# Batch 1's head pairs 2 and 3 transposed by DMA instead of TensorE, with the schedule around them moved

## The chip, the cores and the metric

The kernel runs on one core of one Trainium2 chip. The metric is the device time of one execution in microseconds (us), the median of several runs. The kernel before takes 240.53 us (three runs, 240.4 to 240.64). The profile that is read below is of one execution with a span of 239.1 us.

Engines have these names in the profile: PE is TensorE's matmul, PEld its weight load, DVE is VectorE, ACT is ScalarE, POOL is GpSimd and SP is SyncE. POOL and SP also issue DMA transfers, and each of those queues is worked through in order.

## The reference

An attention with a local window and eight global keys, and behind it a gated feed-forward block over all 3072 tokens.

```python
def _attn_ref(q, k, v, n_global, n_local):
    B, H, S, D = q.shape                      # 4, 8, 768, 64
    scores = np.matmul(q, k.transpose(0, 1, 3, 2)) / np.sqrt(D)
    pos = np.arange(S)
    rel = pos[:, None] - pos[None, :]
    is_global = pos[None, :] < n_global       # the first 8 keys
    is_local = (rel >= 0) & (rel < n_local)   # the last 96 keys up to the query
    keep = is_global | is_local
    dist = np.where(is_global & ~is_local, n_local, np.abs(rel))
    slopes = 2.0 ** (-8.0 * (np.arange(H) + 1) / H)
    scores = scores - slopes[:, None, None] * dist
    scores = np.where(keep, scores, -1e9)
    a = softmax(scores)                       # max, exp, sum written out in the reference
    return np.matmul(a, v)

def _moe_ref(x, w_gate, w_val, w_out):        # x: 3072 x 512, the heads side by side
    g = x @ w_gate                            # 512 x 1536
    return (g / (1 + np.exp(-g)) * (x @ w_val)) @ w_out
```

The inputs and the output are float32; the kernel computes in float16 with float32 sums.

## The kernel before

The feed-forward block is the bulk of the work. It is cut into 8 tiles of 384 tokens, two tiles per batch. A tile has 12 steps f = 0 to 11; each step computes a gate product (`gps`, 4 matmuls) and a value product (`vps`, 4 matmuls), and tanh, two multiplies and a store into `hT` follow on ACT and DVE. The product with `w_out` is cut into "output pieces" of 3 matmuls (`ops`): four pieces make one block of 128 tokens, and the last of the four is followed by ACT's copy and SP's store.

The attention of the next batch is computed between the steps of the current tiles. A head pair needs its queries and keys with the head dimension on the partitions (`qT`, `kT`), so both are transposed. For batch 1 TensorE does that: batches 2 and 3 have it done by DMA.

```python
# the staging of q and k: two layouts, "tokens (p j)" for TensorE, rows for the DMA transpose
    def stage(b):
        qst[b] = sb2.tile([128, H, J * D], FP16, name="qst", tag="qst")
        kst[b] = sb2.tile([128, H, J * D], FP16, name="kst", tag="kst")

    def load_qk(b, h0, h1):
        for st, src in ((kst[b], k), (qst[b], q)):
            nc.gpsimd.dma_start(
                out=st[:, h0:h1, :],
                in_=src[b, h0:h1].rearrange("h (p j) d -> p h (j d)", p=128))

    def stage_rows(b):
        qst[b] = sb2.tile([128, NP, J, 2, D], FP16, name="qst", tag="qst")
        kst[b] = sb2.tile([128, NP, J, 2, D], FP16, name="kst", tag="kst")
        kend[b] = sb2.tile([128, H, D], FP16, name="kend", tag="kend", bufs=1)
        nc.gpsimd.memset(kend[b], 0.0)
        nc.sync.dma_start(out=kend[b][0:NG], in_=kG[:, b - 1])
        for hp in range(NP):
            pair = kG[:, b - 1, 2 * hp:2 * hp + 2, :].rearrange("p h d -> p (h d)")
            nc.sync.dma_start(
                out=kst[b][0:NG, hp].rearrange("p t e d -> p t (e d)"),
                in_=pair.unsqueeze(1).broadcast_to([NG, J, 2 * D]))

    def load_v_rest(b, c):
        n = min(KC, S - KC * c)
        nc.gpsimd.dma_start(
            out=vSs[b][NG:NG + n, c, :, :],
            in_=v[b, :, KC * c:KC * c + n, :].rearrange("h p d -> p h d"))
# ... cut ...
    def load_rows(b, i, h):
        st, src = ((qst, q), (kst, k))[i]
        p0, n = ((0, 128), (NG, KC))[i]
        nc.gpsimd.dma_start(
            out=st[b][p0:p0 + n, h // 2, :, h % 2, :],
            in_=src[b, h, 0:n * J].rearrange("(t p) d -> p t d", p=n))

    def load_ends(b):
        nc.gpsimd.dma_start(
            out=kend[b][NG:NG + S - KC * J],
            in_=k[b, :, KC * J:S, :].rearrange("h p d -> p h d"))

    def turn_ends(b):
        nc.sync.dma_start_transpose(out=kE, in_=kend[b].rearrange("p h d -> p (h d)"))
```

A pair transposed by TensorE (12 transposes for q and 12 for k; copies to SBUF on ACT and DVE), and one transposed by DMA:

```python
        def transposes(self):
            b, hp = self.b, self.hp
            trq, trk = (t[:, 0:S] for t in banks("trs", FP16))
            for st, tr in ((kst[b], trk), (qst[b], trq)):
                for j in range(J):
                    for hi in range(2):
                        nc.tensor.transpose(
                            tr[64 * hi:64 * hi + 64, 128 * j:128 * j + 128],
                            st[:, 2 * hp + hi, D * j:D * j + D], ident)
            self.qT = sb2.tile([128, S], FP16, name="qT", tag="qT", bufs=NP)
            self.kT = kTs[hp]
            k3 = self.kT.rearrange("r (c m) -> r c m", m=128)
            t3 = trk.rearrange("r (j p) -> r p j", j=J)
            for c0, c1, n in ((0, 6, KC), (6, 7, S - 6 * KC)):
                nc.scalar.copy(
                    out=k3[:, c0:c1, NG:NG + n].rearrange("r c (p j) -> r c p j", j=J),
                    in_=t3[:, 20 * c0:20 * c0 + (c1 - c0) * (n // J), :].rearrange(
                        "r (c p) j -> r c p j", c=c1 - c0))
            nc.vector.tensor_copy(
                out=self.qT.rearrange("r (p j) -> r p j", j=J),
                in_=trq.rearrange("r (j p) -> r p j", j=J))
            nc.vector.tensor_copy(
                out=k3[:, :, 0:NG],
                in_=k3[:, 0, NG:2 * NG].unsqueeze(1).broadcast_to([128, NCH, NG]))
# ... cut ...

        def transposes_dma(self):
            b, hp = self.b, self.hp
            self.qT = sb2.tile([128, S], FP16, name="qT", tag="qT", bufs=NP)
            self.kT = kTs[hp]
            for dst, st in ((self.kT[:, 0:S], kst), (self.qT, qst)):
                nc.sync.dma_start_transpose(
                    out=dst.rearrange("r (t p) -> r t p", t=J),
                    in_=st[b][:, hp].rearrange("p t e d -> p (t e d)"))
```

The scores of a pair and the weighted values of four heads, which are called below `sc` and `va`:

```python
            hp = self.hp
            for c in range(NCH):
                cb, col, q0, n = chunks[c]
                if cb != bk:
                    continue
                for hi in range(2):
                    r = slice(64 * hi, 64 * hi + 64)
                    keys = (kE[r, hp, :] if c == J and self.b > 1
                            else self.kT[r, 128 * c:128 * c + 128])
                    nc.tensor.matmul(
                        sc[hi][:, col:col + n], lhsT=keys,
                        rhs=self.qT[r, q0:q0 + n], start=True, stop=True)
        # ... cut: exps (ACT) and mask (DVE or POOL) ...
# ... cut ...

        def x_out(self, half, side):
            return x_of(2 * self.b + half)[:, 2 * self.g + side, :]

        def values(self, half, bank, mul_eng):
            den = bank("den")
            self.weigh(half, den, None)
            srcs = []
            for side in range(2):
            # ... cut: ns copied out on ACT; invert, spread and two scale steps put off to DVE ...
```

The order of the loads on POOL's queue up to batch 1, and the schedule. `(t, f)` names a step of a tile; what stands at `(t, f)` is emitted after the gate, value and output pieces of that step, and `(t, f, n)` before its output piece n.

```python
    for c in range(3, NCH):
        load_v_rest(0, c)
    load_w(wg, 8)
    load_w(wv, 8)
    load_wo(0)
    load_wo(1)
    load_wo(2)
    stage(1)
    load_qk(1, 0, 4)
    load_globals()
    load_wo(3)
    load_qk(1, 4, 8)
    for c in range(NCH):
        load_v_rest(1, c)
# ... cut ...
    def fetch(b, *hps):
        def step():
            for hp in hps:
                pairs[b, hp].transposes_dma()
            if hps[0] > 0:
                turn_ends(b)
        return step

    def first(t, b):
        return {(t, 2): [tr(b, 0), tr(b, 1)],
                (t, 4): [sc(b, (0, 0), (0, 1), (1, 0))],
                (t, 5): [tr(b, 2), tr(b, 3)],
                (t, 6): [sc(b, (1, 1), (2, 0), (2, 1))],
                (t, 8): [sc(b, (3, 0), (3, 1))],
                (t, 9): [va(b, 0, 0)],
                (t, 10, 1): [va(b, 1, 0), lambda: run_later(len(later))]}

    def both(t, b):

        n = b + 1
        return {(t, 0): [sc(b, (0, 2), (1, 2), (2, 2)), fetch(n, 0, 1)],
                (t, 5): [sc(b, (3, 2), (0, 0, n), (1, 0, n)), fetch(n, 2, 3)],
                (t, 8): [vas(b, 1)],
                (t + 1, 0): [sc(n, (0, 1), (1, 1), (2, 0))],
                (t + 1, 4): [sc(n, (2, 1), (3, 0), (3, 1))],
                (t + 1, 8): [vas(n, 0)]}
# ... cut: n_out is the repeating list of how many output pieces a step has ...
    def ff(t, f0, f1, n_out=(0,)):
        return [(t, f, n_out[(f - f0) % len(n_out)]) for f in range(f0, f1)]

    stretches = [
        (ff(0, 9, 10) + ff(0, 10, 12, (1,)), {}),
        (ff(1, 0, 6, (1, 0, 0, 1, 1, 2)) + ff(1, 6, 10, (1, 1, 1, 0)) + ff(1, 10, 12, (2,)), first(1, 1)),
        (ff(2, 0, 12, (1,)) + ff(3, 0, 12, (1,)), both(2, 1)),
        (ff(4, 0, 12, (1,)) + ff(5, 0, 12, (1,)), both(4, 2)),
        (ff(6, 0, 12, (1,)), second(6, 3)),
        (ff(7, 0, 10, (1,)) + ff(7, 10, 12), {})]
# ... cut ...
    at_step(1, 7, lambda: [copy_globals(b) for b in range(1, B)])
    for b, base, rate, v_at in ((2, 20, 2.0, (31, 32, 33, 34, 35, 36, 37)), (3, 38, 1.4, (56, 57, 58, 59, 60, 61, 62))):
        items = [(base, lambda b=b: stage_rows(b)), (base + 1, lambda b=b: load_ends(b))]
        n = 0
        for hp in range(NP):
            for i in (1, 0):
                for e in range(2):
                    items.append((base + n / rate,
                                  lambda b=b, i=i, h=2 * hp + e: load_rows(b, i, h)))
                    n += 1
        items += [(at, lambda b=b, c=c: load_v_rest(b, c)) for c, at in enumerate(v_at)]
        for when, it in items:
            at_step(int(when) // NFF, int(when) % NFF, it)
```

Of the kernel before, what the change touches and what calls it, by code (L numbers as in the profile page):

```python
# [10 lines left out]
FP16 = mybir.dt.float16  # L11
# [26 lines left out]
def kernel(  # L38
# [14 lines left out]
    B, H, S, D = q.shape  # L53
    NG, NL = int(n_global), int(n_local)
    assert (B, H, S, D) == (4, 8, 768, 64)
    assert (NG, NL) == (8, 96)
    NP = H // 2
# [5 lines left out]
    J = S // 128  # L63
    NCH = 7
# [26 lines left out]
    sb2 = ctx.enter_context(tc.tile_pool(name="sb2", bufs=2))  # L91
# [50 lines left out]
    qst, kst, kend = {}, {}, {}  # L142
    kE = sb.tile([128, NP, 128], FP16, name="kE")
# [9 lines that stand above are left out]
                in_=src[b, h0:h1].rearrange("h (p j) d -> p h (j d)", p=128))  # L153

    def stage_rows(b):
        qst[b] = sb2.tile([128, NP, J, 2, D], FP16, name="qst", tag="qst")
        kst[b] = sb2.tile([128, NP, J, 2, D], FP16, name="kst", tag="kst")
        kend[b] = sb2.tile([128, H, D], FP16, name="kend", tag="kend", bufs=1)
        nc.gpsimd.memset(kend[b], 0.0)
        nc.sync.dma_start(out=kend[b][0:NG], in_=kG[:, b - 1])  # L160
        for hp in range(NP):
            pair = kG[:, b - 1, 2 * hp:2 * hp + 2, :].rearrange("p h d -> p (h d)")
            nc.sync.dma_start(
                out=kst[b][0:NG, hp].rearrange("p t e d -> p t (e d)"),
                in_=pair.unsqueeze(1).broadcast_to([NG, J, 2 * D]))

    def load_v_rest(b, c):
# [4 lines that stand above are left out]
# [11 lines left out]
    def copy_globals(b, c0=0):  # L183
        nc.sync.dma_start(
            out=vSs[b][0:NG, c0:],
            in_=vG[:, b, :, :].unsqueeze(1).broadcast_to([NG, NCH - c0, H, D]))


    def load_rows(b, i, h):
        st, src = ((qst, q), (kst, k))[i]  # L190
        p0, n = ((0, 128), (NG, KC))[i]
        nc.gpsimd.dma_start(  # L192
            out=st[b][p0:p0 + n, h // 2, :, h % 2, :],
            in_=src[b, h, 0:n * J].rearrange("(t p) d -> p t d", p=n))

    def load_ends(b):
# [3 lines that stand above are left out]
# [15 lines left out]
    def load_wo(g):  # L215
        nc.gpsimd.dma_start(
            out=wo[:, 3 * g:3 * g + 3, :],
            in_=moe_w_out[384 * g:384 * g + 384].rearrange("(f p) d -> p f d", p=128))
# [18 lines left out]
    def banks(name, dt=FP32):  # L237
        return [bank(name, dt) for _ in range(2)]

    def spare(name, dt=FP32):  # L240
        tag = state["x"][gv.get("n", 0) % len(state["x"])]
        gv["n"] = gv.get("n", 0) + 1
        return single(name, tag, dt)
# [9 lines left out]
    later = []  # L253

    def run_later(n):
        for _ in range(n):
            if later:
                later.pop(0)()

    class Pair:  # L260
# [114 lines left out]
        def scores(self, bk, mul_eng, sc):  # L375
# [4 lines that stand above are left out]
                    continue  # L380
                for hi in range(2):
                    r = slice(64 * hi, 64 * hi + 64)
                    keys = (kE[r, hp, :] if c == J and self.b > 1
                            else self.kT[r, 128 * c:128 * c + 128])
                    nc.tensor.matmul(  # L385
                        sc[hi][:, col:col + n], lhsT=keys,
                        rhs=self.qT[r, q0:q0 + n], start=True, stop=True)
            at = sb2.tile([128, 2, BANK], FP16, name="at", tag=f"at{bk}", bufs=NP)
            self.at[bk] = at

            def exps():
                for hi in range(2):
                    nc.scalar.activation(out=at[:, hi, :], in_=sc[hi][:, 0:BANK],  # L393
                                         func=AF.Exp, scale=scale)

            def mask():
                m = masks[:, 2 * hp:2 * hp + 2, :]
                if bk == 1:
                    for i in range(2):
                        a2 = at[:, :, WIN * i:WIN * i + WIN]  # L400
                        mul_eng.tensor_mul(a2, a2, m[:, :, WIN:2 * WIN])  # L401
                else:
                    o = WIN // 2 * bk
                    mul_eng.tensor_mul(at, at, m[:, :, o:o + BANK])  # L404

            return exps, mask
# [5 lines that stand above are left out]
            for dst, st in ((self.kT[:, 0:S], kst), (self.qT, qst)):  # L412
                nc.sync.dma_start_transpose(
                    out=dst.rearrange("r (t p) -> r t p", t=J),
                    in_=st[b][:, hp].rearrange("p t e d -> p (t e d)"))


    class Quad:
# [192 lines left out]
    for c in range(3):  # L611
        load_v_rest(0, c)
    nc.gpsimd.dma_start(  # L613
        out=vSs[0][NG:NG + cut, 3], in_=v[0, :, 3 * KC:TB, :].rearrange("h p d -> p h d"))
# [80 lines left out]
    load_qk(1, 0, 4)  # L695
    load_globals()
    load_wo(3)
    load_qk(1, 4, 8)
    for c in range(NCH):
        load_v_rest(1, c)  # L700

    gv["n"] = 1
    hb = [bank("gps") for _ in range(4)]
# [5 lines left out]
    def sc(b, *units):  # L709
        def step():  # L710
            for i, (hp, bk, *other) in enumerate(units):
                pair = pairs[b + 1 if other else b, hp]
                on_vector = pair.b < 2 or bk < 2 or hp % 2 == 0
                exps, mask = pair.scores(
                    bk, nc.vector if on_vector else nc.gpsimd,
                    [spare("sc") for _ in range(2)] if i == 0 and len(units) == 3
                    else banks("sc"))
                if i == 0:
                    exps()
                else:  # L720
                    later.append(exps)
                later.append(mask)
        return step

    def va(b, g, half):
        return lambda: quads[b, g].values(half, bank, nc.vector)
# [4 lines left out]
    def tr(b, hp):  # L731
        return pairs[b, hp].transposes
# [23 lines left out]
    def fetch(b, *hps):  # L756
        def step():
            for hp in hps:
                pairs[b, hp].transposes_dma()
            if hps[0] > 0:  # L760
                turn_ends(b)
        return step

    def first(t, b):
        return {(t, 2): [tr(b, 0), tr(b, 1)],
                (t, 4): [sc(b, (0, 0), (0, 1), (1, 0))],
                (t, 5): [tr(b, 2), tr(b, 3)],
                (t, 6): [sc(b, (1, 1), (2, 0), (2, 1))],
                (t, 8): [sc(b, (3, 0), (3, 1))],
                (t, 9): [va(b, 0, 0)],  # L770
                (t, 10, 1): [va(b, 1, 0), lambda: run_later(len(later))]}

    def both(t, b):

# [35 lines left out]
    def ff(t, f0, f1, n_out=(0,)):  # L810
        return [(t, f, n_out[(f - f0) % len(n_out)]) for f in range(f0, f1)]

    stretches = [
        (ff(0, 9, 10) + ff(0, 10, 12, (1,)), {}),
        (ff(1, 0, 6, (1, 0, 0, 1, 1, 2)) + ff(1, 6, 10, (1, 1, 1, 0)) + ff(1, 10, 12, (2,)), first(1, 1)),
        (ff(2, 0, 12, (1,)) + ff(3, 0, 12, (1,)), both(2, 1)),
        (ff(4, 0, 12, (1,)) + ff(5, 0, 12, (1,)), both(4, 2)),
        (ff(6, 0, 12, (1,)), second(6, 3)),
        (ff(7, 0, 10, (1,)) + ff(7, 10, 12), {})]

    loads, after = {}, {}

    def at_step(t, f, *fns):
        loads.setdefault((t, f), []).extend(fns)

    def mask_at(t, f, which, h, c0, c1):
        after.setdefault((t, f, which), []).append(lambda: make_masks(h, c0, c1))

    spots = [(0, f) for f in (8, 9, 10, 10, 11, 11)] + [(1, f // 2) for f in range(10)]
    for n, (t, f) in enumerate(spots):  # L830
        mask_at(t, f, n % 2, n // 2, *((0, WIN), (WIN, 3 * WIN))[n % 2])
    at_step(1, 7, lambda: [copy_globals(b) for b in range(1, B)])
    for b, base, rate, v_at in ((2, 20, 2.0, (31, 32, 33, 34, 35, 36, 37)), (3, 38, 1.4, (56, 57, 58, 59, 60, 61, 62))):
        items = [(base, lambda b=b: stage_rows(b)), (base + 1, lambda b=b: load_ends(b))]
        n = 0
# [103 lines left out]
```

The softmax here doesn't subtract the row's maximum and nothing guards it: scores larger than these inputs give would overflow.

## Time and profile before

| what | value |
|---|---|
| time, median of 3 runs | 240.53 us (240.4 to 240.64) |
| span of the profiled execution | 239.1 us |
| PE busy | 232.8 us |
| DVE, ACT, POOL busy | 168.0, 127.7, 93.9 us |
| granted TensorE clock | 1.0 in every stretch |
| transposes of batch 1 on PE | 96 (48 of `kst`, 48 of `qst`), at 45.4 to 46.9 and 54.2 to 55.8 us |
| DMA transposes of batches 2 and 3 | 8 of `kst`, 8 of `qst`, 2 of `kend` |

In the lines below, a group of instructions is given as line, engine, operation and `output<-input`, with its count and its mean or total time. The chain of work is read from the last instruction back to what released it, and printed in order of time as start, duration, what. A wait is given as "who waited <- for whom: us in total, times, longest". In a timeline the bracket gives the idle time before an entry and what ended it. All times inside the program are us from the start of the span.

### The profile page before, as it was taken

Reading aid. Unit: us, or ns where it says so; the run is one execution under the profiler, and the core shown is the slowest. Engines: PE = TensorE matmul, PEld = TensorE weight load, DVE = VectorE, ACT = ScalarE, POOL = GpSimd, SP = SyncE. Lnnn points to the kernel's source line nnn. Section 1 sums busy time; section 2 is a strip of 40 time slices with the busy share of each in tenths; the row PEclk is TensorE's granted clock in tenths of the full one; section 3 lists DMA queues with packets and bytes.
Section 4 is the critical chain, followed back from the end, with each engine's and each line's share of the span. In section 5 each row is a group of like instructions: output and inputs, shape, how many; then the busy total and the mean of one; then the engine's idle time right before and its main releaser. Section 6 shows DMA issues by size and latency. Waiting matters only on the chain.

```text
span 239.1 us, 6040 instructions
## 1 busy us (share of the span) xinstructions
PE 232.8 (97%) x2424; PEld 134.9 (56%) x2424; DVE 168.0 (70%) x363; ACT 127.7 (53%) x290; POOL 93.9 (39%) x113
## 2 busy tenths in 40 slices
PE   7899999999999999999999999999999999999994
PEld 4565565656555556555655556555655556555543
DVE  6889569978897678676885668776785668555530
ACT  4836776888846365367346365367356435233311
POOL 8976674568970003994082163700031213000000
PEclk9999999999999999999999999999999999999999
DMA  7999999999999446999149649920110110111022
GB/s 140 161 198 201 181 205 204 195 170 154 157 138 135 111 112 91 126 129 122 41 62 112 112 111 133 127 55 2 46 44 3 44 44 3 47 45 44 7 84 88
DMA packets 83332, 25.00 MB, mean 105 GB/s; under 512 B 72600, under 2 KB 80360, under 8 KB 83304
## 3 DMA queue, kind: packets, MB, share of 16 engines
q0 software_dynamic: 64208, 14.05, 64.2%
q1 hardware_dynamic: 18664, 10.36, 17.8%
q8 instruction: 19, 0.31, 0.5%
q10 hardware_dynamic: 432, 0.21, 0.4%
q14 instruction: 9, 0.07, 0.1%
HBM read 28.62 MB, written 6.29 MB: 146 GB/s over the span
## 4 chain that ended last, share of the span: by engine, by line
PE 85%; DMA 10%; POOL 3%; issue 1%; ACT 0%; POOLq 0%
PE ops L585 25%; PE gps L553 25%; PE vps L553 24%; DMA wg<-in_moe_w_gate_dram 10%; PE num L445 3%; PE sc L385 3%; PE den L445 2%; PE trs L272 1%; POOL vS L169 1%; PE ops L601 1%; POOL k L118 1%; POOL q L118 1%; POOL wg L211 0%; POOL vS L613 0%; ACT osb L605 0%
## 5 line engine op out<-in xcount | busy, mean ns | idle before, releaser
L564 ACT ACTIVATE th<-gps 128x384 f32<-128x384 f32 x96 | 47.3, 494 | 63.1 <-PE gps L553 57.3
L569 DVE SCALAR_TENSOR_TENSOR sl<-th,gps 128x384 f32<-128x384 f32 x96 | 52.7, 551 | 38.6 <-ACT th L564 38.0
L553 PE MATMUL gps<-xT,wg 128*128 128x384 f16 x384 | 78.2, 327 | 0.5 <-DVE xT L503 0.3
L553 PE MATMUL vps<-xT,wv 128*128 128x384 f16 x384 | 77.9, 326 | 0.2 <-DMA wv<-in_moe_w_val_dram 0.2
L585 PE MATMUL ops<-wo,hT 128*128 128x512 f16 x276 | 73.1, 379 | 0.0
L573 DVE TENSOR_TENSOR hT<-vps,sl 128x384 f16<-128x384 f32 x96 | 53.0, 554 | 8.2 <-PE vps L553 0.5
L553 PEld LDWEIGHTS <-wg 128*128 128x128 f16 x384 | 35.5, 98 | 32.1 <-issue 2.1
L553 PEld LDWEIGHTS <-wv 128*128 128x128 f16 x384 | 37.1, 98 | 25.6 <-DMA wv<-in_moe_w_val_dram 0.7
L585 PEld LDWEIGHTS <-hT 128*128 128x128 f16 x276 | 26.9, 98 | 23.6
L393 ACT ACTIVATE at<-sc 128x432 f16<-128x432 f32 x72 | 33.8, 534 | 10.2 <-PE sc L385 10.2
L522 POOL TENSOR_TENSOR xT<-ns,rb 128x384 f16<-128x384 f32 x10 | 9.8, 996 | 65.2 <-DVE rb L461 54.3
L169 POOL DMA_DIRECT2D vS<-in_v_dram x28 | 24.7, 891 | 5.5 <-DMA qst<-in_q_dram 1.4
L591 ACT ACTIVATE osb<-ops 128x512 f32<-128x512 f32 x23 | 13.7, 597 | 14.6 <-PE ops L585 14.4
L404 POOL TENSOR_TENSOR at<-at,masks 128x864 f16<-128x864 f16 x4 | 7.3, 1824 | 23.9 <-ACT at L393 19.3
L404 DVE TENSOR_TENSOR at<-at,masks 128x864 f16<-128x864 f16 x20 | 12.2, 609 | 5.6 <-ACT at L393 5.6
L192 POOL DMA_DIRECT2D kst<-in_k_dram x16 | 14.0, 897 | 2.2 <-PE sc L385 1.5
L518 ACT COPY ns<-num 128x384 f32<-128x384 f32 x24 | 9.8, 494 | 9.6 <-PE num L445 9.6
L192 POOL DMA_DIRECT2D qst<-in_q_dram x16 | 13.7, 883 | 0.9 <-DMA qst<-in_q_dram 0.6
L367 ACT ACTIVATE at<-sc 128x432 f16<-128x432 f32 (+2 forms) x32 | 11.4, 460 | 2.5 <-PE sc L356 2.5
L401 DVE TENSOR_TENSOR at<-at,masks 128x432 f16<-128x432 f16 x24 | 8.1, 377 | 4.4 <-ACT at L393 4.4
L445 PE MATMUL num<-at,vS 128*32 128x216 f16 (+6 forms) x576 | 10.9, 224 | 0.0
L455 DVE STREAM_TRANSPOSE dT<-den 128x384 f32<-128x384 f32 x16 | 9.3, 581 | 1.2 <-PE den L445 0.5
(71 smaller groups left out, 165.8 us busy)
## 6 DMA issues: line engine op xcount, KB each, us to landing
out_dram<-osb SPq DMA_DIRECT2D x23, 256.0 KB
vS<-in_v_dram POOLq DMA_DIRECT2D x24, 120.0 KB, 5.6
wg<-in_moe_w_gate_dram POOLq DMA_DIRECT2D x6, 256.0 KB, 7.7
wv<-in_moe_w_val_dram POOLq DMA_DIRECT2D x6, 256.0 KB, 8.1
wo<-in_moe_w_out_dram POOLq DMA_DIRECT2D x4, 384.0 KB, 10.3
qst<-in_q_dram POOLq DMA_DIRECT2D x16, 96.0 KB, 5.2
kst<-in_k_dram POOLq DMA_DIRECT2D x16, 90.0 KB, 5.6
kst<-in_k_dram POOLq DMA_DIRECT2D x2, 384.0 KB, 11.9
```

Source lines behind the costliest of these rows:

```text
L169: nc.gpsimd.dma_start(out=vSs[b][NG:NG + n, c, :, :], in_=v[b, :, KC * c:KC * c + n, :].rearrange("h p d -> p h d"))
L192: nc.gpsimd.dma_start(out=st[b][p0:p0 + n, h // 2, :, h % 2, :], in_=src[b, h, 0:n * J].rearrange("(t p) d -> p t d", p=n))
L367: nc.scalar.activation(out=at[:, hi, 0:col + n], in_=sc[hi][:, 0:col + n], func=AF.Exp, scale=scale)
L393: nc.scalar.activation(out=at[:, hi, :], in_=sc[hi][:, 0:BANK], func=AF.Exp, scale=scale)
L404: mul_eng.tensor_mul(at, at, m[:, :, o:o + BANK])
L445: nc.tensor.matmul(dst[r, o:o + n], lhsT=ones[:, 0:32] if side is None else vals[:, 4 * g + j, side::2], rhs=pairs[b, 2 * g + j // 2].at[c ...
L553: nc.tensor.matmul(gv[f, which][:, 0:TB], lhsT=w[:, c, 128 * f:128 * f + 128], rhs=x_of(t)[:, c, :], start=(c == 0), stop=(c == NC - 1))
L564: nc.scalar.activation(out=th, in_=dst[:, 0:TB], func=AF.Tanh, scale=0.5)
L569: nc.vector.scalar_tensor_tensor(out=sl, in0=th, scalar=1.0, in1=dst[:, 0:TB], op0=AluOp.add, op1=AluOp.mult)
L573: nc.vector.tensor_mul(hTs[t][:, f, :], dst[:, 0:TB], gv.pop(("sl", f)))
L585: nc.tensor.matmul(ops, lhsT=hTs[t][:, f, 128 * i:128 * i + 128], rhs=wo[:, f, :], start=(f == 0), stop=(f == NFF - 1))
L591: nc.scalar.mul(out=osb, in_=ops, mul=0.5)
```

## The change

Pairs 2 and 3 of batch 1 are no longer transposed on TensorE. Their queries and keys are loaded as rows (as those of batches 2 and 3 are) by eight smaller transfers, the last 48 keys of each head go into `kend`, the eight global keys are copied in front of each row block, and SP issues the four transposes and the one of `kend`. Pairs 0 and 1 stay on TensorE. The point is to take 48 of the 96 transposes, and the copies behind them, off TensorE, ACT and DVE.

What had to move with it: V of batch 1 is loaded behind the transpose of the last keys (at step (1, 6), behind a clearing of `kend` for batch 2), not directly behind the weights; the later scores of batch 1 stand one step later, the values one step later, and three output pieces stand behind the second values. Tile 1 thereby has 13 output pieces instead of 12, and tile 7 has 9 instead of 10.

```diff
--- before.py
+++ after.py
@@ -153,15 +153,25 @@
                 in_=src[b, h0:h1].rearrange("h (p j) d -> p h (j d)", p=128))
 
     def stage_rows(b):
-        qst[b] = sb2.tile([128, NP, J, 2, D], FP16, name="qst", tag="qst")
-        kst[b] = sb2.tile([128, NP, J, 2, D], FP16, name="kst", tag="kst")
+        stage(b)
+        if b not in kend:
+            stage_ends(b)
+        rows_globals(b, 0)
+
+    def stage_ends(b):
         kend[b] = sb2.tile([128, H, D], FP16, name="kend", tag="kend", bufs=1)
         nc.gpsimd.memset(kend[b], 0.0)
+
+    def rows_of(st, b, hp):
+        return st[b][:, 2 * hp:2 * hp + 2, :].rearrange("p h x -> p (h x)").rearrange(
+            "p (t e d) -> p t e d", e=2, d=D)
+
+    def rows_globals(b, hp0):
         nc.sync.dma_start(out=kend[b][0:NG], in_=kG[:, b - 1])
-        for hp in range(NP):
+        for hp in range(hp0, NP):
             pair = kG[:, b - 1, 2 * hp:2 * hp + 2, :].rearrange("p h d -> p (h d)")
             nc.sync.dma_start(
-                out=kst[b][0:NG, hp].rearrange("p t e d -> p t (e d)"),
+                out=rows_of(kst, b, hp)[0:NG].rearrange("p t e d -> p t (e d)"),
                 in_=pair.unsqueeze(1).broadcast_to([NG, J, 2 * D]))
 
     def load_v_rest(b, c):
@@ -190,7 +200,7 @@
         st, src = ((qst, q), (kst, k))[i]
         p0, n = ((0, 128), (NG, KC))[i]
         nc.gpsimd.dma_start(
-            out=st[b][p0:p0 + n, h // 2, :, h % 2, :],
+            out=rows_of(st, b, h // 2)[p0:p0 + n, :, h % 2, :],
             in_=src[b, h, 0:n * J].rearrange("(t p) d -> p t d", p=n))
 
     def load_ends(b):
@@ -380,7 +390,7 @@
                     continue
                 for hi in range(2):
                     r = slice(64 * hi, 64 * hi + 64)
-                    keys = (kE[r, hp, :] if c == J and self.b > 1
+                    keys = (kE[r, hp, :] if c == J and (self.b > 1 or hp > 1)
                             else self.kT[r, 128 * c:128 * c + 128])
                     nc.tensor.matmul(
                         sc[hi][:, col:col + n], lhsT=keys,
@@ -412,7 +422,7 @@
             for dst, st in ((self.kT[:, 0:S], kst), (self.qT, qst)):
                 nc.sync.dma_start_transpose(
                     out=dst.rearrange("r (t p) -> r t p", t=J),
-                    in_=st[b][:, hp].rearrange("p t e d -> p (t e d)"))
+                    in_=rows_of(st, b, hp).rearrange("p t e d -> p (t e d)"))
 
 
     class Quad:
@@ -695,9 +705,12 @@
     load_qk(1, 0, 4)
     load_globals()
     load_wo(3)
-    load_qk(1, 4, 8)
-    for c in range(NCH):
-        load_v_rest(1, c)
+    stage_ends(1)
+    for hp in range(2, NP):
+        for i in (1, 0):
+            for e in range(2):
+                load_rows(1, i, 2 * hp + e)
+    load_ends(1)
 
     gv["n"] = 1
     hb = [bank("gps") for _ in range(4)]
@@ -757,18 +770,18 @@
         def step():
             for hp in hps:
                 pairs[b, hp].transposes_dma()
-            if hps[0] > 0:
+            if hps[-1] == (2 if b == 1 else NP - 1):
                 turn_ends(b)
         return step
 
     def first(t, b):
         return {(t, 2): [tr(b, 0), tr(b, 1)],
-                (t, 4): [sc(b, (0, 0), (0, 1), (1, 0))],
-                (t, 5): [tr(b, 2), tr(b, 3)],
-                (t, 6): [sc(b, (1, 1), (2, 0), (2, 1))],
-                (t, 8): [sc(b, (3, 0), (3, 1))],
-                (t, 9): [va(b, 0, 0)],
-                (t, 10, 1): [va(b, 1, 0), lambda: run_later(len(later))]}
+                (t, 4): [sc(b, (0, 0), (0, 1), (1, 0)), fetch(b, 2)],
+                (t, 5): [fetch(b, 3)],
+                (t, 7): [sc(b, (1, 1), (2, 0), (2, 1))],
+                (t, 9): [sc(b, (3, 0), (3, 1))],
+                (t, 10): [va(b, 0, 0)],
+                (t, 11, 1): [va(b, 1, 0), lambda: run_later(len(later))]}
 
     def both(t, b):
 
@@ -812,11 +825,11 @@
 
     stretches = [
         (ff(0, 9, 10) + ff(0, 10, 12, (1,)), {}),
-        (ff(1, 0, 6, (1, 0, 0, 1, 1, 2)) + ff(1, 6, 10, (1, 1, 1, 0)) + ff(1, 10, 12, (2,)), first(1, 1)),
+        (ff(1, 0, 6, (1, 0, 0, 1, 1, 2)) + ff(1, 6, 12, (1, 1, 1, 0, 1, 4)), first(1, 1)),
         (ff(2, 0, 12, (1,)) + ff(3, 0, 12, (1,)), both(2, 1)),
         (ff(4, 0, 12, (1,)) + ff(5, 0, 12, (1,)), both(4, 2)),
         (ff(6, 0, 12, (1,)), second(6, 3)),
-        (ff(7, 0, 10, (1,)) + ff(7, 10, 12), {})]
+        (ff(7, 0, 12, (1, 1, 1, 0)), {})]
 
     loads, after = {}, {}
 
@@ -829,6 +842,9 @@
     spots = [(0, f) for f in (8, 9, 10, 10, 11, 11)] + [(1, f // 2) for f in range(10)]
     for n, (t, f) in enumerate(spots):
         mask_at(t, f, n % 2, n // 2, *((0, WIN), (WIN, 3 * WIN))[n % 2])
+    at_step(1, 0, lambda: rows_globals(1, 2))
+    at_step(1, 6, lambda: stage_ends(2))
+    at_step(1, 6, lambda: [load_v_rest(1, c) for c in range(NCH)])
     at_step(1, 7, lambda: [copy_globals(b) for b in range(1, B)])
     for b, base, rate, v_at in ((2, 20, 2.0, (31, 32, 33, 34, 35, 36, 37)), (3, 38, 1.4, (56, 57, 58, 59, 60, 61, 62))):
         items = [(base, lambda b=b: stage_rows(b)), (base + 1, lambda b=b: load_ends(b))]
```

## The prediction

> **What bounds the kernel now.** I read four views, in this order: the head of the page, the chain of work around the change, the waits of PE, and the timelines of the two queues that issue DMA. The head of the page, and of its slices PE and DMA:
>
> ```profile
> PE 232.8 (97%) x2424; PEld 134.9 (56%) x2424; DVE 168.0 (70%) x363; ACT 127.7 (53%) x290; POOL 93.9 (39%) x113
> ...
> PE   7899999999999999999999999999999999999994
> ...
> DMA  7999999999999446999149649920110110111022
> ```
>
> PE is full from the third slice (12 us) to the last. A busy PE is not proof of a full one, so I looked at its waits alone from 36 us to the end: matmuls have no wait there at all, and weight loads only some 11 us of "issue", which lies beside running matmuls. So after about 33 us each 0.65 us of PE work taken out is 0.65 us of time, unless something PE needs comes late. DMA is full up to 72 us too; that is where the change puts its new traffic. The chain of work from 54 to 72 us:
>
> ```profile
> 54.30 1.46 PE trs L272 x48
> 55.77 0.76 PE gps L553 x4
> 56.52 0.65 PE vps L553 x4
> 57.17 0.65 PE ops L585 x3
> 57.82 0.66 PE sc L385 x12
> ...
> 64.36 0.37 PE den L445 x16
> 64.74 0.55 PE num L445 x32
> 65.28 0.76 PE gps L553 x4
> ...
> 68.26 0.75 PE ops L585 x3
> 69.01 0.65 PE gps L553 x4
> 69.66 0.65 PE vps L553 x4
> 70.31 1.29 PE ops L585 x6
> 71.61 0.49 PE gps L553 x3
> ```
>
> To be seen: every piece follows the last without a gap; the 48 transposes of pairs 2 and 3 are one block of 1.46 us; and the first product after a block of another shape takes 0.76 instead of 0.65 us.
>
> **What the Trainium skill says.** "TensorE: Matmul & The Clock Gate", Part 4 (PE-mode transpose), says that such a transpose lands in PSUM and needs a copy, and gives about 275 ns for one inside a kernel. Here the median is 219 ns as recorded, but they overlap, and a block costs 1.46/48 = 30 ns each; the block is what counts. "DMA: Bandwidth & Descriptors", Specifications, asks for 512 B or more per transfer for full rate. The trace agrees: from 34 to 38 us, with weights, 826 packets moved 0.83 MB; from 54 to 58 us, with rows and V in 128 B pieces, 4226 packets of the software queue moved 0.51 MB. The same page, Rules for kernel authors, says that transfers issued from SP, ACT and GpSimd share the same 16 engines. The trace fits: at 73.5 to 79.5 us the transposes ran with little else, while those of the change run beside row loads. "Perfetto Trace Analysis", Identifying the Most-Contended Engine, warns that matmul busy share is no measure of headroom; hence the look at waits and the gapless chain.
>
> **The change part by part.**
>
> *Removed from PE.* 48 transposes, one block: 1.46 us. The product behind it is then 0.65 instead of 0.76: 0.11 us. Sum 1.57 us, all on the path. ACT loses four copies (1.63 us, 54.80 to 56.43) and DVE about 2.4 us (two copies of 0.95, two small ones): neither is the bound, so nothing for the time.
>
> *Moved on PE.* Scores and values keep their number and their neighbours, and the total of output pieces is unchanged: 0. One piece (0.65 us) moves from tile 7 to tile 1: 0.
>
> *Added behind the second values.* DVE needs, after the last `hT` of tile 1, some 3.5 us to give the last `xT` (before: from 68.12 to 71.63). PE has, from the last value product of tile 1, one piece 0.65, values 0.92 and three pieces 2.05 (first one 0.1 dearer), 3.6 us, and `hT` ends about 0.6 us after that product, while the last quarter of the gate product starts 0.5 us after its first: about even. I put 0.1 us against it.
>
> *The row loads: when do they land?* POOL before:
>
> ```profile
> 35.36 0.78 POOL L216 DMA_DIRECT2D wo<-in_moe_w_out_dram  x1 [0.53 <-DMA wv<-in_moe_w_val_dram]
> 37.24 0.81 POOL L151 DMA_DIRECT2D kst<-in_k_dram  x1 [1.11 <-DMA wo<-in_moe_w_out_dram]
> 39.16 0.75 POOL L151 DMA_DIRECT2D qst<-in_q_dram  x1 [1.11 <-DMA wo<-in_moe_w_out_dram]
> 41.06 0.95 POOL L169 DMA_DIRECT2D vS<-in_v_dram  x1 [1.15 <-DMA wo<-in_moe_w_out_dram]
> 43.01 0.94 POOL L169 DMA_DIRECT2D vS<-in_v_dram  x1 [1.00 <-DMA kst<-in_k_dram]
> 45.34 3.58 POOL L169 DMA_DIRECT2D vS<-in_v_dram  x4 [1.40 <-DMA qst<-in_q_dram]
> ```
>
> Each issue waits for the transfer eight before it. The eight row loads take the places from 37.24 us on, so the eighth is issued at about 48 us and `kend` at 48.9. The last weights (issued 35.36, landing 11.7 us later) land at 47.1, and the rows queue behind them. Eight rows are 4 x 720 + 4 x 768 = 5952 packets; at some 1,100 packets per us (4226 in 4 us at 54 to 58 us, 4560 at 50 to 54 us) that is 5.4 us: the last row lands at 52.5, `kend` (384 packets) at about 53. An output store of 256 KB and the first two transposes run in the same time, so I take 54.4.
>
> *The transposes on SP.* Before, for batch 2:
>
> ```profile
> 73.91 1.32 SPq L413 DMA_TRANSPOSE kT<-kst  x1
> 75.41 1.21 SPq L413 DMA_TRANSPOSE qT<-qst  x1
> 76.84 1.21 SPq L413 DMA_TRANSPOSE kT<-kst  x1
> 78.16 1.22 SPq L413 DMA_TRANSPOSE qT<-qst  x1
> ```
>
> One every 1.4 us; their packets start over 1 us after the issue and run some 1.5 us, so one lands about 2.7 us after its issue. In the changed kernel SP issues the output store (at 49.7), keys and queries of pair 2 (50.1 and 51.5, landing by 54.5), then the transpose of `kend` (54.5, landing 57.2), then pair 3 (55.9 and 57.3, landing by 60). The scores of pair 2 on PE: 54.30 plus steps 6 and 7 (1.95 each) is 58.2; those of pair 3, after 0.66, 2.06 and 1.3 more, at 62.2. Slack 3.7 and 2.2 us: no wait.
>
> *V of batch 1.* POOL clears `kend` only when its transpose has landed: 57.2 to 57.75. Then V at 0.9 us each: the fourth piece, the last that the first values need, is issued at 60.5. V transfers took 3.6 us to land with little traffic (95.6 us) and 4.9 to 5.6 at 68 to 70 us: 64.1 to 66.1. The first values on PE: 62.2 plus the scores 0.6 and step 10 (2.06) is 64.9; `num` starts 0.37 us later and takes the fourth piece at 65.5. So V is the tight spot: from 1.4 us early to 0.6 late in the middle case, and 1.2 us either way for the landing of `kend`. Before, V had landed at 57.2, seven us early. I put a mean stall of 0.3 us.
>
> *Later.* The rows of batch 2 start on POOL at about 63 instead of 51.9 us. The first eight are issued by 71 and land by 76.5; the transposes of batch 2 then land at about 79.5, and PE wants them at about 83: no wait. What comes after is as before.
>
> Sum: 240.53 - 1.57 + 0.1 + 0.3 = 239.4.
>
> **The rivals.**
>
> 1. *V takes the place of the transposes.* If the rows need 0.9 us each instead of 0.7 (at 52 to 68 us the issue pace was 0.87), `kend` lands near 56, and V's fourth piece at 66 to 67.5: a stall of 0.5 to 2 us, time 239.4 to 241. For it: the chain rows, `kend`, its transpose, the clearing, V has no slack, and DMA is full there. Against: V queues behind nothing at 58 us.
>
> 2. *The DMA work is wholly hidden.* 238.9 to 239.0, the full 1.57 us. For it: PE's order has been stretched by a step for both scores and values, which is about what V needs.
>
> 3. *The second values.* The DVE chain to the first gate of tile 2 is exposed by 0.5 to 1 us, because values now stand behind the last gate and only three pieces cover them: 239.9. Against: DVE has 2.4 us less to do there.
>
> 4. *Collision further on.* Output pieces are one ahead in tiles 2 to 6, so the copies of ACT fall just in front of scores and values; a bank released late could cost 0.1 us in several places. Nothing in the waits of PE before says that any bank is near late.
>
> **Range and chances.** The whole gain is bounded by 1.57 us (0.65%), so faster by over 2% has 1%. Slower by over 2% needs a stall of over 6 us, with V or the transposes that much later than worked out: 2%. The middle is 239.4; the low end is the full gain and a little spread, 238.7; the high end a V stall of nearly 3 us, 240.8. A stall is likelier than a larger gain, so the range is longer above.
>
> **What would show it.** PE's `trs` line 48 fewer; no gap in the chain where the block stood (about 54.3); SP's transpose of `kend` issued at 54 to 55 and V's first load at 57 to 58.5; a wait of the `num` matmuls or their weight loads for `vS`, if any, at 65 us; the first gate of tile 2 at 70.8, after one piece more than before; the last value product of tile 7 about 1.9 us earlier (1.2, and the piece moved). The prediction is wrong if scores of pairs 2 or 3 wait for DMA, if the first values stall by more than 2 us, or if batch 2's scores near 83 us wait for rows.

## The result and the profile after

The changed kernel takes 248.0 us (median of 4 runs, 247.45 to 248.09) against 240.58 us before (240.4 to 241.0): a ratio of 1.030, 95% interval 1.028 to 1.032. It is slower by 7.4 us; the prediction of 239.4 us is missed by 8.6.

The head of the page after, and of its slices PE, the granted clock and DMA (40 slices of 6.2 us):

```profile
PE 234.8 (95%) x2376; PEld 134.6 (55%) x2376; DVE 166.6 (68%) x359; ACT 125.7 (51%) x286; POOL 100.3 (41%) x121
...
PE   8979999999989949999999999999999999999994
...
PEclk9999999999999967999999999999999999999999
...
DMA  7999999999999992199918749690110110111022
```

The count of matmuls fell from 2424 to 2376, the 48 transposes. But PE now has a hole, the 4 in the fifteenth slice, at 86 to 92 us, and in that slice and the next the granted clock is at 6 and 7 tenths. The waits of PE after name it, with two smaller ones ("who waited <- for whom: us in total, times, longest"):

```profile
PE sc L395 <- DMA qT<-qst: 3.5, 1, 3.5
...
PE num L455 <- DMA vS<-in_v_dram: 0.7, 2, 0.5
...
PE gps L563 <- DVE xT L491: 0.5, 1, 0.5
```

None of the three is in the kernel before. The first is the scores of batch 2, not of batch 1, whose transposes the change moved. PE's timeline there (start, duration, what):

```profile
86.19 0.36 PE L395 MATMUL sc<-qT,kT 64*128 64x216 f16 x4
90.04 0.54 PE L395 MATMUL sc<-qT,kT 64*128 64x216 f16 x4 [3.49 <-DMA qT<-qst]
90.52 1.46 PE L563 MATMUL gps<-xT,wg 128*128 128x384 f16 x4
...
95.50 0.81 PE L563 MATMUL vps<-xT,wv 128*128 128x384 f16 x4
```

PE stands for 3.5 us, and then a gate product takes 1.46 instead of 0.81 us as recorded: the granted clock fell to 0.5 at about 88.6 us, in the gap, and came back only at 95.4. GpSimd's and SyncE's timelines point to the cause of the late `qT`:

```profile
56.69 0.52 POOL L163 MEMSET kend<- 128x512 f16 x1 [6.71 <-DMA kE<-kend]
57.20 6.07 POOL L179 DMA_DIRECT2D vS<-in_v_dram  x7
63.22 1.72 POOL L202 DMA_DIRECT2D kst<-in_k_dram  x2
...
78.60 2.81 POOL L179 DMA_DIRECT2D vS<-in_v_dram  x3
```

```profile
79.45 1.92 SPq L423 DMA_TRANSPOSE kT<-kst  x1
81.48 1.37 SPq L423 DMA_TRANSPOSE qT<-qst  x1
```

GpSimd waits 6.7 us for the transpose of the last keys, loads V of batch 1, and starts batch 2's rows at 63.2 us instead of 51.9. The rows are issued until 78.6, and the first three loads of V of batch 2 until 81.4: SyncE's four transposes of pairs 0 and 1 (76.45 to 82.9) now run beside them. The last of these was issued at 81.48; the chain of work puts its landing 8.4 us later, at 89.9:

```profile
81.48 8.43 DMA qT<-qst
```

In the kernel before, the software queue (GpSimd's loads; SyncE's transfers are in the hardware queue) was empty by 75 us. What the two DMA queues moved in 2 us, as packets, MB and share of 16 engines, first at 86 to 88 us after, then at 77 to 79 us before, when the transposes had the engines to themselves:

```profile
q0 software_dynamic: 1277, 0.15, 125.3%
q1 hardware_dynamic: 620, 0.15, 67.1%
```

```profile
q1 hardware_dynamic: 1268, 0.31, 80.2%
```

Beside the software queue the transposes get half their packets here.

The loss in the profile, place by place. The first transposes of batch 1 stand at 46.40 us against 45.41 before: 1.0 us from waits for the first weights. The other changed kernels share all code up to there, and have it at 44.6 to 45.5, one at 46.5, so this is the spread of single executions. The first value product of tile 2 stands at 73.94. Before it stood at 72.26; with the 1.0 us, less 1.57 for the transposes, plus 0.65 for the moved piece, it should be at 72.33: 1.6 us are lost at the waits for `vS` (0.7) and `xT` (0.9). The values of tile 2 start 8.1 us later than before (98.84 against 90.73), so 6.4 us more are lost between: the gap of 3.5 and the slow clock behind it. The moved piece gives back 0.65 later.

### The profile page after: what moved, and what is told of

It is laid out like the page before. It is cut to its first block, busy times and chain, and to the rows that moved or that the text cites. A ratio compares the mean times of both kernels' runs of the same rounds, so it can differ in the third digit from the quotient of the medians.

```text
span 246.3 us, 5965 instructions
## 1 busy us (share of the span) xinstructions
PE 234.8 (95%) x2376; PEld 134.6 (55%) x2376; DVE 166.6 (68%) x359; ACT 125.7 (51%) x286; POOL 100.3 (41%) x121
## 4 chain that ended last, share of the span: by engine, by line
PE 74%; DMA 17%; POOL 4%; DVE 2%; issue 1%; ACT 0%; POOLq 0%; SPq 0%; DVEq 0%
PE gps L563 22%; PE vps L563 21%; PE ops L595 21%; DMA wg<-in_moe_w_gate_dram 10%; DMA qT<-qst 3%; PE num L455 3%; DMA vS<-in_v_dram 3%; PE sc L395 3%; POOL vS L179 2%; PE den L455 2%; PE ops L611 1%; DMA kE<-kend 1%; DVE xT L491 1%; POOL k L118 1%; POOL q L118 1%
## 5 line engine op out<-in xcount | busy, mean ns | idle before, releaser
L579 DVE SCALAR_TENSOR_TENSOR sl<-th,gps 128x384 f32<-128x384 f32 x96 | 52.9, 552 | 45.5 <-ACT th L574 44.9
L563 PE MATMUL gps<-xT,wg 128*128 128x384 f16 x384 | 79.7, 331 | 1.7 <-DMA wg<-in_moe_w_gate_dram 1.1
L563 PE MATMUL vps<-xT,wv 128*128 128x384 f16 x384 | 78.6, 329 | 0.5 <-DMA wv<-in_moe_w_val_dram 0.5
L403 ACT ACTIVATE at<-sc 128x432 f16<-128x432 f32 x72 | 33.2, 540 | 5.1 <-PE sc L395 5.1
L532 POOL TENSOR_TENSOR xT<-ns,rb 128x384 f16<-128x384 f32 x10 | 9.8, 997 | 62.5 <-ACT ns L528 31.5
L202 POOL DMA_DIRECT2D kst<-in_k_dram x20 | 17.6, 897 | 3.1 <-DMA wo<-in_moe_w_out_dram 1.6
L202 POOL DMA_DIRECT2D qst<-in_q_dram x20 | 17.2, 881 | 2.9 <-DMA wo<-in_moe_w_out_dram 1.1
L395 PE MATMUL sc<-qT,kT 64*128 64x216 f16 (+2 forms) x148 | 9.4, 252 | 3.6 <-DMA qT<-qst 3.5
```

What stands on the lines that cost most here:

```text
L202: nc.gpsimd.dma_start(out=rows_of(st, b, h // 2)[p0:p0 + n, :, h % 2, :], in_=src[b, h, 0:n * J].rearrange("(t p) d -> p t d", p=n))
L395: nc.tensor.matmul(sc[hi][:, col:col + n], lhsT=keys, rhs=self.qT[r, q0:q0 + n], start=True, stop=True)
L563: nc.tensor.matmul(gv[f, which][:, 0:TB], lhsT=w[:, c, 128 * f:128 * f + 128], rhs=x_of(t)[:, c, :], start=(c == 0), stop=(c == NC - 1))
L579: nc.vector.scalar_tensor_tensor(out=sl, in0=th, scalar=1.0, in1=dst[:, 0:TB], op0=AluOp.add, op1=AluOp.mult)
```

## The experiments

Theory A: batch 2's rows start 11 us later on GpSimd's queue, so they and V of batch 2 run beside batch 2's transposes, the last of these lands late, and PE stands and loses its clock. Rival B: the loss lies in what the change did on purpose, the DMA transposes of batch 1 or the moved scores, values and pieces. The kernel before ran beside each (240.6 to 240.8 us).

**V of batch 1 ahead of the clearing.**

```diff
-    at_step(1, 6, lambda: stage_ends(2))
     at_step(1, 6, lambda: [load_v_rest(1, c) for c in range(NCH)])
+    at_step(1, 6, lambda: stage_ends(2))
```

> The changed kernel with one thing undone: V of batch 1 is issued ahead of the clearing of kend, so it no longer waits for the transpose of the last keys, and the rows of batch 2 follow the clearing directly. Theory A (the loss comes from batch 2's rows starting 11 us later on GpSimd's queue, at 63.2 instead of 51.9 us, so that they and V of batch 2 run beside the transposes of batch 2, of which the last lands late): the rows start near 57 us, the wait of the scores for qT (3.5 us) and the fall of the clock behind it are gone, as is the 0.5 us wait for V; 239 to 240.5 us. Rival B (the loss lies in the DMA transposes of batch 1 or in the later scores, values and output pieces): 246 us or more.

244.0 us, ratio 1.014 (1.013 to 1.016): neither. The rows were to start near 57 us; they started at 62.5. One line of GpSimd's timeline and one of PE's waits of this run:

```profile
61.64 0.53 POOL L163 MEMSET kend<- 128x512 f16 x1 [6.60 <-issue]
```

```profile
PE sc L395 <- DMA qT<-qst: 4.1, 4, 1.6
```

V of batch 1, issued at 48.9 to 55.0, now ran beside batch 1's transposes, and they crawled: from 55 to 61 us the hardware queue moved 530 to 650 packets in 2 us (1593 at 54 to 56 us in the changed kernel). The transpose of `kend`, issued at 53.27, took up to 8.3 us, where it took 2.5 in the changed kernel (54.10 to 56.59). That its landing ends the 6.60 us is inferred: the line names no releaser, but the clearing overwrites what this transpose reads. So the clearing, and the rows behind it, came no sooner, and PE waited for transposes of batch 1 as well as of batch 2. The order that looked like the fault is what kept V out of the way of batch 1's transposes.

**V of batch 2 later.** Its first three loads go behind GpSimd's scaling of the values of tile 2 (at 95.6 us in this run), where the other four were.

```diff
-    for b, base, rate, v_at in ((2, 20, 2.0, (31, 32, 33, 34, 35, 36, 37)), ...
+    for b, base, rate, v_at in ((2, 20, 2.0, (35, 35, 35, 36, 36, 37, 37)), ...
```

> The changed kernel with all seven loads of V of batch 2 behind GpSimd's scaling in tile 3, so that none of them is in the queue at 78 to 90 us; batch 2's rows still start at 63 us. Theory A1 (the transposes of batch 2 are issued in time but crawl because V of batch 2 and the last rows share the DMA engines with them): the wait for qT shrinks from 3.5 to under 1.5 us and with it the fall of the clock; 241 to 244 us. Rival A2 (the transposes are late because the rows themselves arrive late, V of batch 2 has no part in it): 247 to 248 us.

241.8 us, ratio 1.004 (1.002 to 1.006). 6.2 of the 7.4 us come back with three transfers moved, the rows as late as before. The wait for `qT` is 0.8 us, and the clock stays at 1.0. A1 holds.

**The kernel before with late rows.** 21 clearings of a scratch tile on GpSimd ahead of batch 2's rows, nothing of the change.

```diff
+        if b == 2:
+            items = [(base, idle_pool)] + items     # 21 x nc.gpsimd.memset(scratch, 0.0)
```

> The kernel before, with 21 clearings of a scratch tile on GpSimd (some 11 us) ahead of the rows of batch 2: nothing else of the change. Theory A (the later rows of batch 2 alone make the loss): a wait of the scores for the transposes near 84 us, a fall of the clock, 245 to 248 us. Rival B (the DMA transposes of batch 1, or the moved scores and values, make it): 240.5 to 241.5 us.

244.75 us, ratio 1.016 (1.014 to 1.019), slightly under the range of A: the wait is 2.1 us, with half clock behind it. The line of PE's waits:

```profile
PE sc L385 <- DMA qT<-qst: 2.1, 1, 2.1
```

Without anything else of the change, late rows cost the old kernel 4.0 us, so B can't be the whole of the 7.4. The changed kernel adds to it: its last transpose is issued 3.2 us later than here (81.48 against 78.29), and 1.6 us are lost at `vS` and `xT`.

**The same, with V of batch 2 later.** Both edits above on the kernel before.

> The kernel before with the rows of batch 2 late by some 11 us (scratch clearings, as in the run before_rows_late, 244.75 us), and now V of batch 2 behind GpSimd's scaling. Theory A1 (V of batch 2, which with late rows falls beside the transposes, is what makes them crawl): 240.5 to 241.5 us. Rival A2 (late rows of pairs 2 and 3 beside the transposes of pairs 0 and 1 are enough): 243.5 to 245 us.

240.8 us, ratio 1.000 (0.998 to 1.002), no wait for `qT`. With rows 10.5 us late (62.4 against 51.9) but V of batch 2 out of the way, nothing is lost. This separates the two: the rows' delay matters because it pushes V of batch 2 into the transposes.

**The kernel before with more V beside the transposes.** The rows on time, all seven loads of V of batch 2 right behind them.

```diff
-    ... ((2, 20, 2.0, (31, 32, 33, 34, 35, 36, 37)), ...
+    ... ((2, 20, 2.0, (31, 31, 31, 31, 31, 31, 31)), ...
```

> The kernel before with all seven loads of V of batch 2 directly behind its rows, so that four more of them (from some 70.7 to 74.3 us on GpSimd's queue) are in the queue when SyncE transposes batch 2 from 73.9 us on. The rows themselves are on time. Theory A1 (a transpose crawls beside any load of the software queue in 128 B pieces): the transposes of pairs 0 and 1 slow down to 4 to 8 us; their traffic is spread to 84 us instead of ending at 81, and TensorE may wait 0 to 2 us at 84 us: 240.5 to 243 us. Rival A3 (it needs late rows as well): their traffic ends at 81 us as before, 240.3 to 240.9 us.

240.7 us, ratio 1.000 (0.998 to 1.001), no wait at 84 us. The time lies in both ranges; that the traffic of the transposes ends at 81 us is A3's, and A1 as I had put it, for any load alongside, was too strong. The two queues at 75 to 77 us, then the hardware queue at 77 to 79:

```profile
q0 software_dynamic: 2016, 0.24, 189.4%
q1 hardware_dynamic: 345, 0.09, 55.2%
...
q1 hardware_dynamic: 1642, 0.40, 102.8%
```

Beside 2016 packets of the software queue the transposes moved 345; when that queue ran dry at 77 they moved 1642 in the next 2 us. So they are slow while the software queue runs, and catch up once it is dry. In these runs the loss follows the time at which it runs dry: 77 us here and 81 in the run before this one (no wait), some 85 with late rows and V (last landing 86.6), and 88 in the changed kernel (89.9).

**The gap filled.** 32 matmuls of ones, overwritten by the scores behind them, where PE waits.

```diff
+            if (self.b, hp, bk) == (2, 1, 0):
+                for _ in range(32):
+                    nc.tensor.matmul(sc[0][:, 0:256], lhsT=ones[:, 0:128],
+                                     rhs=ones[:, 0:256], start=True, stop=True)
```

> The changed kernel with 32 matmuls of ones (256 columns, overwritten by the scores that follow) put into TensorE's queue where it waits 3.5 us for qT of batch 2. They add no wait, only keep TensorE busy. Theory C (of the loss, some 2.7 us are the clock that falls to half after the gap and stays there for about 5 us): the clock stays at 1.0, 245 to 245.7 us. Rival D (the gap itself is all that costs, the clock would have been made up for elsewhere): 247.5 to 248.5 us.

245.8 us, ratio 1.021 (1.018 to 1.023): 2.2 us less than the changed kernel, just short of C's 2.3 to 3.0, with the gap filled by 3.6 us of work that does nothing. The stretches 84 to 90 and 90 to 96 us, first of the changed kernel, then of this (PE, PEld, DVE, ACT, POOL busy, then the granted clock, DMA share, GB/s):

```profile
84.00:90.00 6.00, 2.41 (x20) 1.10 (x18) 2.28 (x4) 1.88 (x4) 0.00 (x0) 0.88 1.86 174
90.00:96.00 6.00, 5.96 (x23) 2.71 (x24) 1.63 (x3) 2.48 (x6) 0.00 (x0) 0.55 0.79 138
```

```profile
84.00:90.00 6.00, 6.00 (x56) 4.18 (x55) 2.00 (x4) 1.51 (x4) 0.00 (x0) 1.00 1.72 169
90.00:96.00 6.00, 6.00 (x61) 3.30 (x62) 4.09 (x8) 3.32 (x8) 0.00 (x0) 1.00 0.92 133
```

From 90 to 96 us PE is busy all the time in both, with 23 matmuls against 61; 28 of the 61 are short ones of `den`, so 23 compare with 33. The busy share hides half a clock.

**Scores later.** The scores of pair 1 of batch 2 go from step (2, 5) to (3, 0), with the others shifted behind them; loads and transposes stay as in the changed kernel.

```diff
+        steps[t, 5] = [sc(b, (3, 2), (0, 0, n)), fetch(n, 2, 3)]
+        steps[t + 1, 0] = [sc(n, (1, 0), (0, 1), (1, 1))]
+        steps[t + 1, 4] = [sc(n, (2, 0), (2, 1), (3, 0))]
+        steps[t + 1, 6] = [sc(n, (3, 1))]
```

> The changed kernel with the scores of pair 1 of batch 2 moved from step (2, 5) to step (3, 0), so that nothing needs the late qT until some 12 us later; loads and transposes are untouched and stay as late as they were. Theory A (the loss is TensorE standing at one wait for a late transpose, and the clock that falls behind it): both are gone, 241 to 242.5 us, at most as fast as the run with V of batch 2 later (241.8). Rival E (the crowded DMA queues cost TensorE at other places too, the wait only shows them first): 244 us or more.

241.9 us, ratio 1.005 (1.003 to 1.008). With the transposes as late as ever (a `qT` issued at 78.18 took 9.1 us), 6.1 us come back. Even the scores of pair 0 wait now, 1.2 us. So the loss was one wait and the clock behind it, not crowded queues everywhere.

**Five pieces behind the second values**, on top of V of batch 2 later; tile 7 gives up one.

```diff
-  ff(1, 6, 12, (1, 1, 1, 0, 1, 4)) ... (ff(7, 0, 12, (1, 1, 1, 0)), {})
+  ff(1, 6, 12, (1, 1, 1, 0, 1, 5)) ... (ff(7, 0, 12, (1, 1, 0)), {})
```

> The run with V of batch 2 later, and five instead of four output pieces behind the last value product of tile 1 (tile 7 has one less). Theory F (the first gate product of tile 2 waits 0.5 to 0.8 us for the last xT, because the second values stand too close before it): that wait is gone and the piece fills its place, 240.7 to 241.4 us against 241.8. Rival G (the wait is set by V's landing and only moves on): no change, 241.6 to 242 us.

244.9 us, ratio 1.019 (1.016 to 1.022): slower, and foreseen by neither. The wait for `xT` behind the second values (L491) did go; a new line leads PE's waits:

```profile
PE ops L595 <- DVE hT L583: 3.8, 5, 0.8
```

Five waits of some 0.75 us, one in each of tiles 2 to 6. With the pieces two ahead of the kernel before, the last piece of a block, which needs the twelfth `hT`, stands directly behind the product that this `hT` comes from.

**All together**: the same, with scores later, and the global values of batches 2 and 3 copied behind tile 2's transposes.

> All of it together: V of batch 2 later, scores of pair 1 of batch 2 later, five output pieces, and the copies of the global values of batches 2 and 3 behind tile 2's transposes. If the three waits (qT 0.8, xT 0.5 to 0.8, part of vS) are all that is left of the loss, the 1.57 us of the transposes come through: 239.3 to 240.3 us. If other costs are left: 240.7 to 241.5 us.

244.9 us, ratio 1.018 (1.014 to 1.023), above both ranges: the same five waits. Those for `qT`, `vS` and the second values' `xT` are all gone.

**One ahead.** As the last, but the fifth piece comes from step (2, 2), and tile 7 keeps its nine.

```diff
-  ... (ff(2, 0, 12, (1,)) + ff(3, 0, 12, (1,)), ...
+  ... (ff(2, 0, 12, (1, 1, 0) + 9 * (1,)) + ff(3, 0, 12, (1,)), ...
```

> The run e7_together, but with the fifth piece behind the last value product of tile 1 taken from step (2, 2) and not from tile 7, so that the output pieces run one ahead of the kernel before, as in the changed kernel, and not two. Theory H (the 3.8 us that e6 and e7 lost are the last piece of each of tiles 2 to 6 waiting some 0.75 us for its last hT, because two pieces ahead puts it directly behind that hT): these waits are gone, TensorE waits for nothing but 0.3 us, and the removed transposes come through: 239.3 to 240.3 us. Rival I (with the loads moved, something else takes their place): 241 us or more.

239.9 us, ratio 0.996 (0.995 to 0.998): H holds, and this version beats both kernels, the one before by 0.7 us. The PE slices of its page have no hole:

```profile
PE   7899999999999999999999999999999999999994
```

**The same without moving the scores.**

> The same without moving the scores of pair 1 of batch 2. If the rows of pairs 2 and 3 alone still slow the last transpose of pairs 0 and 1 (0.8 us of wait in e2_v2_later): 0.5 to 1.5 us above e9_one_ahead. If V of batch 2 was all of it: within 0.4 us of e9_one_ahead.

240.9 us, ratio 1.001 (0.999 to 1.003), 1.0 us above the last run, with a wait of 1.3 us for `qT`: the rows of pairs 2 and 3, which still run beside the transposes of pairs 0 and 1, cost that much; V of batch 2 was most of it, not all. In the kernel before with late rows and V later (240.8 us) they cost nothing: there the software queue ran dry at 81 us, here at about 83.5.

## Why the prediction was wrong

**The step that failed** is the one under "Later": the transposes of batch 2 "land at about 79.5, and PE wants them at about 83: no wait", and "What comes after is as before". The start of the rows was right (63 predicted, 63.2), and so was the issue of the first eight (71 against 72). The transposes were not. The 79.5 was too early by my own lines: before, the last of the four was issued at 78.16, which with 2.7 us is 80.9; after, it was issued at 81.48. With 2.7 us it would still have landed at 84.2, ahead of the 86.5 at which PE wanted it. The term that failed is the 2.7: I gave it to each transpose, read from a stretch where they had the engines to themselves, although I had written under the skill that these ran with little else and those of the change would not. And I followed only the rows, not the three loads of V of batch 2 behind them, which slid from 68 to 70.7 us into 78.6 to 81.4. Measured: the last took 8.4 us, PE waited 3.5. Moving those three loads gave 6.2 us. The wait came at the last of the signs named beforehand, batch 2's scores near 83 us.

"DMA: Bandwidth & Descriptors", Queues, rings and completion order, of the Trainium skill says that each DMA engine takes turns between the queues that have work, packet by packet. The traces agree that both queues move side by side, but not in equal counts: 620 packets of transposes beside 1277 of the software queue in the changed kernel, 345 beside 2016 in the run with more V. I had cited that page for the shared engines and not drawn the conclusion. That turn-taking is what slows them is not shown; the runs show the rates and the landing.

**The clock** was in no part of the prediction. I took a wait to cost its length. "TensorE: Matmul & The Clock Gate", Part 1, of the skill says that an idle TensorE falls to half its clock and needs sustained work to get it back, and gives about 3.4 us for either. The trace differs from both figures: in the changed kernel the clock fell some 2 us after the last matmul and came back 5.4 us after work resumed. In the kernel before with late rows the gap was 2.1 us; the clock fell at 87.4, 0.7 us after work had resumed, and came back at 90.8. Filling the gap of the changed kernel was worth 2.2 us.

**V of batch 1** was rightly called the tight spot, and its chain held to within 0.6 us: transpose of `kend` issued at 54.1 (predicted 54.5) and landed at 56.6 (57.2), first load of V at 57.2 (57.75). The term mis-sized was its landing: the fourth load took 6.9 us, not 3.6 to 5.6, and `num` waited until 66.9.

**The second values** I sized at 0.1 us, with "`hT` ends about 0.6 us after that product". The product ended at 68.6, and DVE's `sl`, which that `hT` needs too, only at 69.2; then the timeline has DVE spreading the first four heads' reciprocals (0.57 us, at 69.12) in front of it. So `hT` ended at 70.1, 1.5 us after the product, and the last `xT` at 73.6. This and V together lost 1.6 us, where the sum had 0.4. It is rival 3, which I had set aside.

**What was right**: the block of transposes taken off PE with nothing in its place; no wait for the transposes of batch 1's pairs 2 and 3 in the changed kernel, and a bound on the gain. Of the 1.57 us, 0.7 are in the best version; one more block of scores takes 0.1 (the first product behind a block). Some 0.4 us more go before the first value product of tile 2: it stands at 72.45 in that version's chain, where the 72.26 of before, 0.07 for its later first transposes, less 1.57, plus 1.30 for two pieces, give 72.06. What the rest went to was not tried apart. Rival 1 named the right kind of loss at the wrong place, and rival 4 gave no wait with the pieces one ahead; two ahead cost 3.8 us, for `hT` and not for a bank.

## What to carry to other kernels

When a change makes an in-order load queue longer or later, follow everything behind it on that queue, to the end, and ask of each transfer what it now runs beside. Read a transfer's time from a stretch as crowded as the one it will run in. And count a gap on TensorE of some two microseconds at more than its length.

## What the runs showed of the hardware

- DMA transposes of head pairs took 5.7 to 9.1 us to land with loads in 128 B pieces in the software queue (8.4 us in the changed kernel, 5.7 with V of batch 2 later, 9.1 with scores later). That of `kend` took 2.5 us without such loads beside it, and up to 8.3 with V of batch 1 beside it. The transposes caught up once that queue was dry (345 packets in 2 us, then 1642).
- A gap of 2.1 us on TensorE was followed by half a clock for 3.4 us (late rows in the kernel before); four waits of at most 1.6 us, 4.1 in all (V of batch 1 ahead of the clearing), were not.
